# Adding the key tiles of the last three groups in float32 ahead of one float32 product

## The chip, the cores and the metric

The kernel runs on one core of a Trainium2 chip. The metric is the device time of one execution in microseconds (us); smaller is better. A core has TensorE (PE in the profile, with its weight loads as PEld), VectorE (DVE), ScalarE (ACT), GpSimd (POOL) and SyncE (SP). SP only issues DMAs here; POOL computes and issues DMAs.

## The reference

A cosine attention over 8 batches, 12 heads, 448 positions and 64 dimensions, followed by a two-layer network over the 3584 tokens:

```python
q_n = q / (np.linalg.norm(q, axis=-1, keepdims=True) + 1e-06)
k_n = k / (np.linalg.norm(k, axis=-1, keepdims=True) + 1e-06)
scores = np.matmul(q_n, k_n.transpose(0, 1, 3, 2)) / tau       # tau = 0.1
attn = np.exp(scores - np.max(scores, axis=-1, keepdims=True))
attn = attn / (np.sum(attn, axis=-1, keepdims=True) + 1e-09)
x = np.matmul(attn, v)                                         # to (3584, 768)
h = x @ w_in                                                   # 768 -> 2048
out = np.maximum(0.01 * h, h) @ w_out                          # 2048 -> 768
```

The kernel needs no maximum: the scores are bounded, and numerator and denominator carry the same factor. What this document turns on is the denominator, np.sum(attn): for each query the sum of the exps over all 448 keys.

## The kernel before, in words

**Slots, pairs, units, groups.** Two heads of one batch form a pair (48 pairs). The first 12 pairs (two batches) are done in an older way, in a part of the program written out by hand. From pair 12 on the work goes by *units*: a unit is two pairs, so four heads, and there are 18 of them. Units are gathered into ten *groups* of one or two units (line 186). The last three groups, 7, 8 and 9, are the units 12 and 13, 14 and 15, 16 and 17.

**A unit's key tiles.** A unit's 448 keys are cut into 7 tiles of 64. `quad_tiles` (line 406) makes one tile of scores with eight matmuls (L417), each on a strip of 64 rows by 32 columns of PE's array, into two PSUM banks; ScalarE takes the exp (L423) and writes a bf16 tile `pq[u, i]` of 128 x 2 x 448.

**Sums and products of a group.** `group_products(g, e)` (line 427) multiplies the exps of a group into two PSUM banks. With e = 0 or 1 the weights are columns of v, and the result is half of the attention's numerator. With e = None the weights are ones, and the result is the denominator. In each case there are 7 key tiles x 4 strips x 2 halves = 56 matmuls of 64x32 (L442), which accumulate over the tiles. `group_logs` (L451) and `group_inverse` (L454) turn the sums into reciprocals by way of a log and an exp on ScalarE, and `group_scale` (L467) multiplies the products by them on VectorE, into `xT`, the network's input.

**Visits.** The loop from line 892 on walks through the stream of all 18 x 7 = 126 key tiles, three in a *visit*, so 42 visits (0 to 41). A visit issues, in this order: the normalisation of one slot of a later unit (`normalise`, L253 to L260, on VectorE); its preparation; one key tile; a group's sums or products, if one is due; the other two key tiles; the load of the next group's v (`load_vq`, L202, two DMAs on POOL's queue); then matmuls of the network ("feed": `first`, L494, with its activation on ScalarE, L505, and `second`, L531, with its copy on VectorE, L541, and the DMA to the output), with `roots` of the next slot (L245, L246, ScalarE) ahead of the last piece of the feed. A group's sum comes in the visit after its last key tile, its two products in the two visits after that. Group 9 ends with the last visit, so its sum and its products stand behind the loop (lines 944 to 954), followed by the rest of the network.

**The preparation** (`prepare`, line 897) is: the transposition of the slot just normalised (L306, VectorE, then DMAs from SP), the load of a slot four further on (SP), then on POOL `hold` (L616, a copy of one column of the slot just normalised, which makes POOL wait for VectorE's L260) and `squares` of the slot two further on (L216, POOL), then on VectorE `sums` of the slot one further on (L232), which reads the squares that POOL made in an earlier visit. In visits that carry an e = 0 or 1 product the preparation stands behind that product.

**What sets the order.** The schedule is manual: each engine executes its instructions in the order of the program, and waits where one needs a result of another. The amount of feed in a visit comes from a small planner (lines 880 to 943) that counts the matmul columns of the network and of the e = 0 and 1 products. The eight PSUM banks are dealt in turn (`banks`, line 75): two for each key tile and each sum or product, one for each piece of the feed.

Of the kernel before, what the change touches and what calls it, by code (L numbers as in the profile page):

```python
# [8 lines left out]
F32 = mybir.dt.float32  # L9
BF16 = mybir.dt.bfloat16  # L10
AF = mybir.ActivationFunctionType
ALU = mybir.AluOpType
# [4 lines left out]
def kernel(  # L17
# [10 lines left out]
    nc = tc.nc  # L28
    B, H, S, D = q.shape
# [8 lines left out]
    NSLOT = B * NPAIR  # L38
    NQ = NPAIR // 2
# [8 lines left out]
    ctx.enter_context(tc.manual_schedule())  # L48
    cpool = ctx.enter_context(tc.tile_pool(name="consts", bufs=1))
    ldp = ctx.enter_context(tc.tile_pool(name="ld", bufs=4))  # L50
    vbp = ctx.enter_context(tc.tile_pool(name="vb", bufs=3))
    smp = ctx.enter_context(tc.tile_pool(name="small", bufs=3))
    qnp = ctx.enter_context(tc.tile_pool(name="qn", bufs=3))
    ttp = ctx.enter_context(tc.tile_pool(name="tt", bufs=2))
# [11 lines left out]
    gp = nc.gpsimd  # L66
# [8 lines left out]
    def banks(count, keep=None):  # L75
        lo, hi = (0, 8) if not deals["apart"] else (0, 4) if count == 2 else (4, 8)
        x = min(
            (i for i in range(lo, hi, count) if not set(range(i, i + count)) & set(kept.values())),
            key=lambda i: max(age[i : i + count]),
        )  # L80
        deals["n"] += 1
        age[x : x + count] = [deals["n"]] * count
        if keep:
            kept[keep] = x
        return ps[:, x] if count == 1 else ps[:, x : x + count]
# [26 lines left out]
    def main(x, b, h0, nh):  # L112
        return x[b, h0 : h0 + nh, 0:MAIN].rearrange("h (p t) d -> p h t d", t=3)
# [5 lines left out]
    def halves(x, w=D):  # L119
        return (  # L120
            x[:, 0 : 8 * w].rearrange("p (h t d) -> p h t d", h=2, d=w),
            x[:, 8 * w : 14 * w].rearrange("p (h t d) -> p h t d", h=2, d=w),
        )
# [45 lines left out]
    vb, vrb = {}, []  # L169

    def load_v(j):
        if j >= B * NQ:
            return
        b, jj = divmod(j, NQ)
        vb[j] = vbp.tile([128, 4, 3, D], BF16, name="v_b")
        gp.dma_start(out=vb[j], in_=main(v, b, 4 * jj, 4))

    def load_v_rem(b, heads=range(4)):
# [7 lines left out]
    GROUPS = [(6,), (7, 8), (9, 10), (11,)] + [(j, j + 1) for j in range(12, 24, 2)]  # L186
    assert [j for g in GROUPS for j in g] == list(range(NEWQ, B * NQ))
    UNITS = [
        (g, (2 * js[0] + x, 2 * js[-1] + x if len(js) == 2 else 2 * js[0] + 1))
        for g, js in enumerate(GROUPS) for x in range(len(js))  # L190
    ]
    vq = {}

    def load_vq(g):
# [14 lines left out]
    def squares(s, eng=gp, parts=(0, 1)):  # L209
        if s >= NSLOT:  # L210
            return
        sq = sqt[s % 3]
        if s >= OLD:
            sqs[s] = sq
            x = raw[s].rearrange("p (t d) -> p t d", d=D)
            gp.tensor_tensor(sq[:, :, :D], x, x, op=ALU.mult)  # L216
            return
        sqs[s] = halves(sq.rearrange("p t d -> p (t d)"), D + 1)
        for i in parts:
            x, y = raw[s][i], sqs[s][i]  # L220
            if eng is nc.scalar:
                nc.scalar.activation(y[..., :D], x, func=AF.Square)
            else:
                eng.tensor_tensor(y[..., :D], x, x, op=ALU.mult)  # L224

    def sums(s, parts=(0, 1)):
        if s >= NSLOT:
            return
        if s not in ss:
            ss[s] = smp.tile([128, 14], F32, name="ss")  # L230
        if s >= OLD:
            nc.vector.tensor_reduce(  # L232
                ss[s], sqs[s], axis=AX.X, op=ALU.add
            )
            return
        for i in parts:
            o = ss[s][:, 0:8] if i == 0 else ss[s][:, 8:14]
            nc.vector.tensor_reduce(  # L238
                o.rearrange("p (h t) -> p h t", h=2), sqs[s][i], axis=AX.X, op=ALU.add
            )  # L240
# [7 lines left out]
    qn = {}  # L248
# [80 lines left out]
    def pe_tile():  # L329
        return pep.tile([128, 2, S], BF16, name="pe")  # L330
# [71 lines left out]
            given_back((j, e))  # L402

    pq = {}

    def quad_tiles(which):

        tiles = []
        for u, i in which:
            sc = banks(2)  # L410
            tiles.append(sc)
            for strip in range(4):
                x = qkT[UNITS[u][1][strip // 2]]
                c0 = S + 64 * i + 32 * (strip % 2)
                for a in range(2):
                    rows = slice(64 * a, 64 * a + 64)
                    nc.tensor.matmul(  # L417
                        out=sc[32 * strip : 32 * strip + 32, a, :S], lhsT=x[rows, c0 : c0 + 32],
                        rhs=x[rows, 0:S], start=True, stop=True,
                    )  # L420
        for (u, i), sc in zip(which, tiles):
            pq[u, i] = pe_tile()
            nc.scalar.activation(out=pq[u, i], in_=sc[:, :, :S], func=AF.Exp, scale=inv_tau)  # L423
# [3 lines left out]
    def group_products(g, e):  # L427


        us = [u for u, (gg, _) in enumerate(UNITS) if gg == g]  # L430
        two = len(us) == 2
        po = banks(2)
        for i in range(7):
            for strip in range(4):
                for w in range(2):
                    x, a = strip // 2, strip % 2
                    rows = slice(64 * w, 64 * w + 64)
                    weights = ones[rows] if e is None else (
                        vq[g][rows, strip if two else a, i]
                        .rearrange("p (d e) -> p e d", e=2)[:, e if two else w ^ x]  # L440
                    )
                    nc.tensor.matmul(  # L442
                        out=po[32 * strip : 32 * strip + 32, w, :S],
                        lhsT=weights, rhs=pq[us[x if two else 0], i][rows, a, :],
                        start=(i == 0), stop=(i == 6),
                    )
        return po

    def group_logs(g, po):
        grb[g] = rbp.tile([128, 2, S], F32, name="rb")  # L450
        nc.scalar.activation(grb[g], po[:, :, :S], func=AF.Ln)  # L451

    def group_inverse(g):
        nc.scalar.activation(grb[g], grb[g], func=AF.Exp, scale=-1.0)  # L454
# [133 lines left out]
    nc.vector.memset(warm, 1.0)  # L588
    ones = cpool.tile([128, 32], BF16, name="ones")
    nc.vector.memset(ones, 1.0)  # L590
    ones_rem = cpool.tile([128, 2, 32], BF16, name="ones_rem")
    nc.vector.memset(ones_rem, 0.0)
    for i in range(2):
        nc.vector.memset(ones_rem[64 * i : 64 * i + 64, i], 1.0)
    for i in range(2):
        vrb.append(cpool.tile([128, NQ, 4, D], BF16, name=f"v_rem{i}"))
        nc.vector.memset(vrb[i], 0.0)
    id128 = cpool.tile([128, 128], BF16, name="id128")
    make_identity(nc, id128)
# [15 lines left out]
    def hold(x):  # L615
        gp.tensor_copy(out=seen, in_=x)  # L616
# [35 lines left out]
    for s in range(NPAIR):  # L652
        j = s // 2 - 1 if s >= 2 else None
# [39 lines left out]
        if s in (1, 2):  # L693
            load_v(s)
# [52 lines left out]
    s, j = NPAIR, NQ - 1  # L747
# [3 lines left out]
    po = banks(2)  # L751
# [135 lines left out]
        for n in range(len(visits))  # L887
    ]

    held = []  # L890
    fed = 0
    for n, tiles in enumerate(visits):
        s = preps.get(n, NSLOT)
        g, e = parts.get(n, (None, None))
        scaling = e is not None

        def prepare():
            if s < NSLOT:
                transposes(s)
                load_qk(s + 4)  # L900
                hold(qn[s][:, 6, 0, 0:1])
                squares(s + 2)
                sums(s + 1)

        normalise(s)
        if not scaling:
            prepare()
        quad_tiles(tiles[:1])
        if g is not None:
            po = group_products(g, e)  # L910
            if e is None:
                group_logs(g, po)
            else:
                group_scale(g, e, po)
        if scaling:
            prepare()
        quad_tiles(tiles[1:])
        if g is not None and e is None:
            group_inverse(g)
        for u, i in tiles:  # L920
            if i == 6 and u and UNITS[u][0] != UNITS[u - 1][0]:
                load_vq(UNITS[u][0])
        for c in marked:
            if at[c] == n:
                held += marked[c]
        level = min(
            (sum(loads[c] for c in loads if at[c] <= x) - fed + sum(side[n : x + 1])) / (x - n + 1)
            for x in range(n, len(visits))
        )
        share = (level - side[n]) / (4 if n == len(visits) - 1 else 1)  # L930
        now, done = [], 0
        while held:
            w = weight(held[0][0], held[0][1][0])
            if now and done + w / 2 > share:
                break
            now.append(held.pop(0)[1][1])
            done += w
        fed += done
        for fn in now[:-1]:
            fn()  # L940
        roots(s + 1)
        for fn in now[-1:]:
            fn()
    g = len(GROUPS) - 1
# [47 lines left out]
```

## Time and profile before

| what | value |
|---|---|
| median of 3 runs | 417.24 us (416.48 to 417.70) |
| the profiled execution: its own time | 416.43 us |
| the profiled execution: its span | 414.6 us |
| granted clock of PE | 1.00 |
| visits 28 to 41, by the chain | 245.5 to 344.3 us of the span |
| sum of group 7, 8, 9: start, duration in the chain | 278.19, 1.32; 314.67, 1.32; 344.27, 1.45 us |
| L423, one exp of a key tile (ScalarE) | 915 ns |
| L442 with ones: all 560 matmuls, busy | 15.1 us |
| POOL busy, 245.5 to 277.9 us | 8.5 of 32.4 us |

Times inside the profile count from the start of the span; the execution's own time is 1.8 us longer than its span. A line of the page's table of groups reads: code line, engine, operation, output and inputs, shape and count, then busy time and mean duration of one, then the idle time of that engine just before. The chain that ended last is found by going back from the last instruction, at each step to whatever released it; a piece of the chain is given by start, duration, engine and line. Matmuls are pipelined, so their single durations overlap, and the chain's pieces tell more about the rate.

### The profile page before, as it was taken

Reading aid. Unit: us, or ns where it says so; the run is one execution under the profiler, and the core shown is the slowest. Engines: PE = TensorE matmul, PEld = TensorE weight load, DVE = VectorE, ACT = ScalarE, POOL = GpSimd, SP = SyncE. Lnnn points to the kernel's source line nnn. Section 1 sums busy time; section 2 is a strip of 40 time slices with the busy share of each in tenths; the row PEclk is TensorE's granted clock in tenths of the full one; section 3 lists DMA queues with packets and bytes.
Section 4 is the critical chain, followed back from the end, with each engine's and each line's share of the span. In section 5 each row is a group of like instructions: output and inputs, shape, how many; then the busy total and the mean of one; then the engine's idle time right before and its main releaser. Section 6 shows DMA issues by size and latency. Waiting matters only on the chain.

```text
span 414.6 us, 11342 instructions
## 1 busy us (share of the span) xinstructions
PE 407.1 (98%) x4799; PEld 212.3 (51%) x4799; DVE 221.5 (53%) x387; ACT 250.2 (60%) x431; POOL 114.6 (28%) x149
## 2 busy tenths in 40 slices
PE   8899999999999999999999999999999999999997
PEld 3335555544555555544455555554445555654565
DVE  6977976855778556766474964464621301210022
ACT  5997876378657785668865688547764464004300
POOL 4875543433234132413331433122210000000000
PEclk9999999999999999999999999999999999999999
DMA  7999998775377851884275681742442100020022
GB/s 195 242 214 220 210 234 187 181 223 129 60 206 182 204 132 22 204 229 99 53 186 157 151 229 43 175 126 84 91 90 68 51 39 3 38 77 0 2 76 76
DMA packets 41964, 53.82 MB, mean 130 GB/s; under 512 B 12474, under 2 KB 32314, under 8 KB 41914
## 3 DMA queue, kind: packets, MB, share of 16 engines
q1 hardware_dynamic: 25738, 41.01, 35.0%
q0 software_dynamic: 15488, 11.80, 19.7%
q8 instruction: 37, 0.61, 0.6%
q10 hardware_dynamic: 688, 0.30, 0.2%
q14 instruction: 13, 0.11, 0.1%
HBM read 45.61 MB, written 11.01 MB: 137 GB/s over the span
## 4 chain that ended last, share of the span: by engine, by line
PE 87%; DMA 4%; ACT 3%; DVE 3%; POOL 2%; SPq 1%; issue 1%; POOLq 0%
PE ps L531 34%; PE ps L494 34%; PE ps L442 9%; PE ps L417 7%; ACT pe L355 2%; DMA qk_h<-in_k_dram 2%; PE ps L366 2%; DVE qn L270 1%; DMA xT<-in_k_dram 1%; DMA xT<-in_q_dram 1%; POOL sq L224 1%; PE ps L346 1%; POOL sq L216 1%; DVE ss L238 0%; SPq L131 0%
## 5 line engine op out<-in xcount | busy, mean ns | idle before, releaser
L531 PE MATMUL ps<-w_out_sb,hT 128*128 128x384 bf16 (+1 forms) x912 | 151.3, 324 | 0.3 <-DVE xT L397 0.3
L494 PE MATMUL ps<-xT,w_in_sb 128*128 128x384 bf16 (+1 forms) x768 | 151.1, 353 | 0.0
L423 ACT ACTIVATE pe<-ps 128x896 bf16<-128x896 f32 x126 | 108.9, 915 | 46.1 <-PE ps L417 46.1
L531 PEld LDWEIGHTS <-hT 128*128 128x128 bf16 x912 | 86.5, 98 | 64.3 <-issue 10.0
L494 PEld LDWEIGHTS <-w_in_sb 128*128 128x128 bf16 x768 | 72.6, 98 | 74.3 <-issue 9.7
L505 ACT ACTIVATE hT<-ps 128x384 bf16<-128x384 f32 (+1 forms) x128 | 67.4, 552 | 56.0 <-PE ps L494 55.0
L541 DVE COPY osb<-ps 128x384 f32<-128x384 f32 (+1 forms) x57 | 31.2, 548 | 100.7 <-PE ps L531 100.6
L216 POOL TENSOR_TENSOR sq<-qk_h 128x896 f32<-128x896 f32 x36 | 61.0, 1695 | 9.2 <-DMA qk_h<-in_k_dram 7.7
L616 POOL CAST seen<-qn 128x1 f32<-128x1 bf16 x46 | 8.5, 185 | 169.4 <-DVE qn L260 160.5
L260 DVE TENSOR_TENSOR qn<-qk_h,r 128x896 bf16<-128x896 f32 x36 | 42.4, 1176 | 1.2
L232 DVE TENSOR_REDUCE ss<-sq 128x14 f32<-128x910 f32 x36 | 38.0, 1054 | 1.1 <-POOL sq L216 1.1
L355 ACT ACTIVATE pe<-ps 128x896 bf16<-128x896 f32 x42 | 35.9, 917 | 1.8 <-PE ps L346 1.7
L417 PE MATMUL ps<-qkT 64*32 64x448 bf16 x1008 | 36.5, 353 | 0.0
L253 DVE TENSOR_REDUCE r<-norms 128x14 f32<-128x28 f32 x48 | 8.6, 178 | 48.3 <-ACT norms L246 47.7
L467 DVE TENSOR_TENSOR xT<-ps,rb 128x448 bf16<-128x448 f32 x32 | 18.4, 617 | 23.2 <-PE ps L442 21.5
L306 DVE STREAM_TRANSPOSE tt<-qn 128x448 f32<-128x448 f32 x36 | 29.6, 821 | 0.9
L442 PE MATMUL ps<-pe,vq 64*32 64x448 bf16 x1008 | 27.0, 349 | 0.0
L245 ACT ACTIVATE ss<-ss 128x14 f32<-128x14 f32 x48 | 10.3, 214 | 25.4 <-DVE ss L232 24.4
L417 PEld LDWEIGHTS <-qkT 64*32 64x32 bf16 x1008 | 13.1, 91 | 19.2 <-issue 14.5
L442 PEld LDWEIGHTS <-vq 64*32 64x32 bf16 x1008 | 14.5, 92 | 8.0 <-issue 0.3
L442 PE MATMUL ps<-pe,ones 64*32 64x448 bf16 x560 | 15.1, 349 | 0.0
L346 PE MATMUL ps<-qkT 64*64 64x448 bf16 (+1 forms) x132 | 12.9, 359 | 2.1 <-ACT pe L355 1.2
(53 smaller groups left out, 218.9 us busy)
## 6 DMA issues: line engine op xcount, KB each, us to landing
qk_h<-in_q_dram SPq DMA_DIRECT2D x36, 224.0 KB, 4.0
qk_h<-in_k_dram SPq DMA_DIRECT2D x36, 224.0 KB, 4.3
out_dram<-osb SPq DMA_DIRECT2D x20, 384.0 KB, 2.3
qkT<-tt SPq DMA_DIRECT2D x72, 56.0 KB, 3.3
qkT<-tt SPq DMA_DIRECT2D x36, 112.0 KB, 3.5
vq<-in_v_dram POOLq DMA_DIRECT2D x16, 224.0 KB, 5.0
w_in_sb<-in_moe_w_in_dram POOLq DMA_DIRECT2D x4, 768.0 KB, 11.2
w_out_sb<-in_moe_w_out_dram POOLq DMA_DIRECT2D x2, 1536.0 KB, 22.3
```

What stands on the lines that cost most here:

```text
L216: gp.tensor_tensor(sq[:, :, :D], x, x, op=ALU.mult)
L232: nc.vector.tensor_reduce(ss[s], sqs[s], axis=AX.X, op=ALU.add)
L260: nc.vector.tensor_tensor(qn[s].rearrange("p m d e -> p m e d"), raw[s].rearrange(f"p ({t[1:-1]} d) -> p m e d", e=n, d=D), r.rearrange(f" ...
L306: nc.vector.transpose(out=to.rearrange(("p g (c m) -> p m g c", "p g (m c) -> p m g c")[which], m=7), in_=qn[s].bitcast(F32).rearrange("p ...
L355: nc.scalar.activation(out=dst, in_=sc[:, :, :S], func=AF.Exp, scale=inv_tau)
L417: nc.tensor.matmul(out=sc[32 * strip : 32 * strip + 32, a, :S], lhsT=x[rows, c0 : c0 + 32], rhs=x[rows, 0:S], start=True, stop=True,)
L423: nc.scalar.activation(out=pq[u, i], in_=sc[:, :, :S], func=AF.Exp, scale=inv_tau)
L442: nc.tensor.matmul(out=po[32 * strip : 32 * strip + 32, w, :S], lhsT=weights, rhs=pq[us[x if two else 0], i][rows, a, :], start=(i == 0), ...
L494: nc.tensor.matmul(out=pm[:, :n], lhsT=w_in_sb[:, kt, m * 128 : (m + 1) * 128], rhs=xT[c // 2][:, kt, c0 : c0 + n], start=(done + i == 0), ...
L505: nc.scalar.activation(out=hT[c][:, m, :n], in_=pm[:, :n], func=AF.Prelu, alpha=0.01)
L531: nc.tensor.matmul(out=po2[:, : hi - lo], lhsT=hT[c][:, m, ts * 128 : (ts + 1) * 128], rhs=w_out_sb[:, m, half * HALF + lo : half * HALF + ...
L541: nc.vector.tensor_copy(out=o[:, cols], in_=po2[:, : hi - lo])
```

## The change

For the last three groups the denominator is no longer accumulated over seven key tiles by PE. The seven exp tiles of a unit are first added up element by element into one float32 tile `whole[u]` (128 x 2 x 448): six adds a unit, on GpSimd for units 12, 13 and 14 and on VectorE for units 15, 16 and 17. Then eight float32 matmuls, one for each strip and half, multiply this tile by float32 ones.

The adds of a visit's key tiles are issued behind its last two key tiles; the first add of a unit waits until the group of the unit two before is summed, since there are two float32 tiles. In the visits that carry adds, `hold` and `squares` move behind the adds. To make room, the v tiles of the old part and the two float32 tiles share one buffer, and the float32 ones are written over the identity matrix, which is no longer used then. `ADDED` is 7 and `BY_VECTOR` 15.

```diff
-    vbp = ctx.enter_context(tc.tile_pool(name="vb", bufs=3))
...
-        vb[j] = vbp.tile([128, 4, 3, D], BF16, name="v_b")
+        vb[j] = v_old[:, j % 3]
...
+    ADDED = len(GROUPS) - 3
+    BY_VECTOR = len(UNITS) - 3
...
+    whole, due, summed = {}, [], set()
+
+    def add_up():
+        for u, i in list(due):
+            if i == 1:
+                if UNITS[u - 2][0] >= ADDED and UNITS[u - 2][0] not in summed:
+                    return
+                whole[u] = sum_of[u % 2]
+            due.remove((u, i))
+            eng = gp if u < BY_VECTOR else nc.vector
+            eng.tensor_tensor(
+                whole[u], pq[u, 0] if i == 1 else whole[u], pq[u, i], op=ALU.add
+            )
...
         po = banks(2)
+        if e is None and g >= ADDED:
+            summed.add(g)
+            for strip in range(4):
+                for w in range(2):
+                    rows = slice(64 * w, 64 * w + 64)
+                    nc.tensor.matmul(
+                        out=po[32 * strip : 32 * strip + 32, w, :S], lhsT=ones_f[rows],
+                        rhs=whole[us[strip // 2]][rows, strip % 2, :], start=True, stop=True,
+                    )
+            return po
...
+    shared = cpool.tile([128, 3840], BF16, name="shared")
+    v_old = shared[:, :2304].rearrange("p (j h t d) -> p j h t d", j=3, t=3, d=D)
+    sum_of = [
+        shared[:, 1792 * i : 1792 * (i + 1)].bitcast(F32).rearrange("p (a c) -> p a c", c=S)
+        for i in range(2)
+    ]
...
-        vrb.append(cpool.tile([128, NQ, 4, D], BF16, name=f"v_rem{i}"))
+        lo = 2304 + 768 * i
+        vrb.append(shared[:, lo : lo + 768].rearrange("p (j g d) -> p j g d", g=4, d=D))
...
+    ones_f = id128.bitcast(F32)[:, 0:32]
+    nc.vector.memset(ones_f, 1.0)
...
+        adding = [(u, i) for u, i in tiles if i and UNITS[u][0] >= ADDED]
...
-                hold(qn[s][:, 6, 0, 0:1])
-                squares(s + 2)
+                if not adding:
+                    hold(qn[s][:, 6, 0, 0:1])
+                    squares(s + 2)
                 sums(s + 1)
...
         quad_tiles(tiles[1:])
+        due += adding
+        add_up()
+        if adding and s < NSLOT:
+            hold(qn[s][:, 6, 0, 0:1])
+            squares(s + 2)
```

## The prediction

> **What bounds the kernel.** I read the page's busy shares first, then the chain that ended last, then what TensorE (PE) waited for.
>
> ```profile
> PE 407.1 (98%) x4799; PEld 212.3 (51%) x4799; DVE 221.5 (53%) x387; ACT 250.2 (60%) x431; POOL 114.6 (28%) x149
> ...
> PE 87%; DMA 4%; ACT 3%; DVE 3%; POOL 2%; SPq 1%; issue 1%; POOLq 0%
> ```
>
> PE is busy in 98% of the span and carries 87% of the chain. All that PE ever waited for another engine is this:
>
> ```profile
> PE ps L605 <- DVE pe L588: 1.7, 1, 1.7
> PE ps L346 <- ACT pe L355: 1.2, 5, 0.3
> PE ps L346 <- DVE qkT L325: 0.8, 1, 0.8
> PE ps L284 <- DVE qn L270: 0.6, 2, 0.4
> PE ps L531 <- DVE xT L397: 0.3, 1, 0.3
> ```
>
> None of these lines belongs to the visits (L417, L442): from the first visit on, PE never waits. So there a microsecond of PE is a microsecond of time, and another engine costs something only if it becomes late enough to make PE wait. The chain in order of time (start, duration, what) shows one visit that sums a group, and the stage after the last visit:
>
> ```profile
> 277.88 0.31 PE ps L417 x8
> 278.19 1.32 PE ps L442 x56
> 279.51 0.38 PE ps L417 x16
> ...
> 334.41 9.86 PE ps L494 x60
> 344.27 1.45 PE ps L442 x56
> 345.71 4.01 PE ps L494 x24
> ...
> 354.55 15.60 PE ps L531 x96
> ```
>
> The x56 pieces at 278.19 and 344.27 are sums over the key tiles (weights of ones) of groups 7 and 9; group 8's lies at 314.67, 1.32 us too. From these pieces come two rates. Seven rounds of eight matmuls, each on its own 64x32 strip of the array, take 1.32: eight strips side by side take **0.189 us** for 448 columns. And 96 matmuls of 384 columns that all use the same 128x128 array take 15.60, so 0.1625 each, 0.423 ns a column, which is again 0.189 for 448. So strips that differ run beside each other, and matmuls on one and the same piece of the array follow one another at full streaming time, their weight loads (98 ns each in L531's row) hidden.
>
> **What goes from PE.** Three sums of 56 matmuls: 3 x 1.32 = 3.96 us. All of it is on the chain.
>
> **What comes to PE.** Three times eight float32 products of 64 rows, 32 weights, 448 columns. The built program has 4679 matmuls for 4799: 168 go and 48 come, so each float32 product is two pairs of weight load and matmul. They stand product by product, both matmuls of one product on the same strip, then the next strip. No row of this trace has a float32 matmul, so I bound P, the time of the sixteen. Below: all sixteen at the bf16 pace of strips side by side, 16 x 0.189 / 8 = 0.38. Above: none beside another, and each with twice the bytes. A bf16 column is 2 bytes per row, a float32 one is 4; at L442's bytes per time one matmul takes 2 x 0.189 = 0.379, and sixteen 6.06. The value I take lies between and follows from the two rates above and the order in the program: the second matmul of a product waits for the first, being on its strip (0.379); the next strip's first may run beside it; but its second must wait for its own first. Eight steps of 0.379 and one more to drain: **P = 9 x 0.379 = 3.41 us**. That rests on matmuls starting in program order.
>
> The Trainium skill, "TensorE: Matmul & The Clock Gate" (Part 3, "What overlaps and what doesn't"), says that matmuls start and end strictly in program order; by it the pairs chain as above. Its page "TensorEngine Tiling (Array Packing)" (Key Properties) says that tiles operate independently and in parallel; read to the letter, that gives rival B below. No row of this trace has two matmuls of one small strip in succession, so neither is settled here.
>
> Sum for PE: 3 x (3.41 - 1.32) = **+6.27 us**.
>
> **What comes to GpSimd (POOL).** Eighteen adds for units 12, 13 and 14 (six each). No row has this add; the nearest is the square, L216, a two-input operation on 128x896: 1.68 us in these visits. Below that I have 1.04 for 512 elements (L224), above it this:
>
> ```profile
> 62.02 1.17 DVE L260 TENSOR_TENSOR qn<-qk_h,r 128x896 bf16<-128x896 f32 x1
> 62.53 2.16 POOL L216 TENSOR_TENSOR sq<-qk_h 128x896 f32<-128x896 f32 x1 [3.64 <-DMA qk_h<-in_k_dram]
> 66.26 1.68 POOL L216 TENSOR_TENSOR sq<-qk_h 128x896 f32<-128x896 f32 x1 [1.44 <-DMA qk_h<-in_q_dram]
> ```
>
> The columns are start, duration, engine and line (in brackets, POOL's idle time before). The square at 62.53 began while VectorE (DVE) multiplied two inputs, and took 2.16 where an undisturbed one takes 1.68. Range 1.04 to 2.16; I take 1.68. The Trainium skill, "SBUF — State Buffer" (Who interferes with whom), has a DVE instruction with two SBUF inputs and a GpSimd instruction that reads SBUF block one another; the 0.48 us here agrees in kind, and it speaks against the change, since now the adds run under L260, whereas the squares stood behind it.
>
> Do the adds hold PE up? Group 7's product (278.19) needs unit 12 for its first eight matmuls and unit 13 for the rest, which by my chain begin 4 x 0.379 later, at 279.7. POOL works in order. Unit 13's first add can start when the exps of visit 30 are done, about 265.2 (three exps of 0.9 beginning at 261.5, with two waits). Then follow: one add (to 266.9), the two vq loads (1.27, to 268.2), three adds (to 273.2), the hold and square of visit 31 (0.18 + 1.68, to 275.1), two adds (to 278.5). That is 1.2 us early. The cover is gone when an add takes over 1.9 us; beyond that each 0.1 us costs PE 0.6. At 2.16 it would be 279.7 against 281.3, a stall of 1.6. So I cost it at **nothing**. It happens once only: unit 14 is summed five visits on.
>
> **What moves.** In visits 28, 29 and 31 to 34 hold and square now stand behind two or three adds, which wait for the exps of their own visit. The tightest is the square of visit 31, which ends at 270.1 in the trace and about 275.1 then: DVE's L232 reads it in visit 32's preparation (274.65), so L232 slips some 0.5 us, and with it ScalarE's roots (275.74) and the copy L541 queued behind (275.63). The roots' reader, L253, comes at 278.39: 2 us are left. The vq loads slip from 258.0 to about 267 and land 5 us later; their first reader is the product at 288.1. SP's queue has the same order as before. So nothing again: the cover is these gaps, and without them L541 and the exps would hold PSUM banks and so PE.
>
> **What comes to DVE.** Eighteen adds at L260's 1.18 (two float32 SBUF inputs, the same 896 elements): 21 us from visit 35 on, where DVE is busy little (16.2 of 36.5 us from 277.9 to 314.4, and 5.7 of 29.9 from there to 344.3, by the table of stretches). The adds wait for exps, and behind them wait L541 and L467. The last visit's three exps end at 336.6, so the last add near 338; its product comes at 344.27, behind 9.86 us of L494. Group 8's last add ends near 311 for a product at 314.67. **Nothing.** The first part of the kernel keeps its order and waits; the memset of the float32 ones is one DVE instruction of under 0.1 us.
>
> **The sum.** The profiled execution took 416.43 (span 414.6 and 1.8 around it); with 6.27 it is 422.7. The median of the runs shown, 417.24, is 0.81 above that execution, so for a median I predict **423.5**.
>
> **Rivals.** A measurement of this kernel can tell about 0.3% (1.25 us) from no change.
>
> A, as forecast: P between 3.0 (the eight first matmuls hidden, 8 x 0.379) and 4.24 (a weight load of 0.092 added to each of nine steps): 417.24 + 5.1 to + 8.8, so 422.4 to 426.0. For it: L531's one-after-another rate and the order in the program. Chance 0.58.
>
> B, the other side: different strips run ahead of one another, so that the sixteen overlap eight by eight. Place: the three products. P = 2 x 0.379 = 0.76, price 3 x (0.76 - 1.32) = -1.7, so 415.6. It turns to a gain where P is under 1.32. For it: L442 keeps eight strips full; against: there each strip's next matmul comes eight instructions later, here at once. Chance 0.20.
>
> C, bytes do not count, only columns, and pairs chain: P = 9 x 0.189 = 1.70, +1.2, so 418.4. Chance 0.07.
>
> D, float32 matmuls do not run beside others at all: P = 6.06, +14.2, so 431.5. For it: nothing in the trace; against it only that L442's do. Chance 0.10.
>
> E, the change adds what A does, and POOL's adds last 2.16: PE waits 1.6 at group 7, so 425.1. For it: the row at 62.53; against: L260 is 1.18 in visits of 6 us. Chance 0.05.
>
> Slower: A, D, E, 0.73. Same: C, 0.07. Faster: B, 0.20. The range goes from B to the top of A, 415.3 to 426.5, and leaves out D. A's own range is 422.4 to 426.0.
>
> **What would show it.** Right: three pieces of about 3.4 us in the chain where 1.32 stood, the second matmul of a product starting 0.38 after its first; no PE wait for POOL or DVE; POOL adds of 1.7. Wrong: pieces under 1.3 us (B) or of 6 (D); a PE wait at 278 released by POOL (E); PE waits at L417 or L531 after 265 for banks, which would mean that late squares or waiting adds block L541 or the roots.

## The result and the profile after

The change takes 420.49 us (median of 6 executions, 419.29 to 421.14) against 416.94 before (six executions, the three shown ahead of the forecast among them): ratio **1.0071**, 95% interval 1.0054 to 1.0088. That is 3.0 us by the ratio of the executions (3.55 between the two medians). It is slower, as forecast, but by about half of the 6.3 us forecast, and for other reasons. Two later measurements of the same kernel gave 1.0033 (1.0011 to 1.0055) and 1.0046 (1.0029 to 1.0063).

The busy shares and the chain of the changed kernel (in its listing L452 is the float32 product, L416 the adds, L431 the key tiles, L466 the bf16 products, L518 and L555 the network, L565 its copies, L261 the normalisation):

```profile
span 417.5 us, 11153 instructions
...
PE 404.6 (97%) x4663; PEld 210.6 (50%) x4679; DVE 243.2 (58%) x406; ACT 250.5 (60%) x431; POOL 151.5 (36%) x167
...
PE 81%; DVE 5%; POOL 4%; DMA 4%; ACT 3%; issue 2%; SPq 1%; POOLq 0%; DVEq 0%
```

PE is busy 2.5 us less than before (407.1), yet the span is 2.9 us longer: PE did less and waited more. POOL, 2% of the chain before, is 4% now. (The page lacks the records of 16 of the 4679 matmuls.) What PE waited for, in total, times, longest:

```profile
PE ps L452 <- POOL shared L416: 1.9, 1, 1.9
PE ps L636 <- DVE pe L612: 1.7, 1, 1.7
PE ps L285 <- DVE qn L271: 1.4, 1, 1.4
PE ps L347 <- ACT pe L356: 1.2, 5, 0.3
PE ps L555 <- DVE r L255: 1.2, 1, 1.2
...
PE ps L518 <- DVE osb L565: 0.3, 1, 0.3
```

The first line is new and lies where the forecast had no cost: group 7's product waits for GpSimd's adds. The last is new too. The wait of 1.2 at L555 lies ahead of the visits (below). The chain at the sums of groups 8 and 9, which do not wait for an add:

```profile
317.84 0.31 PE ps L431 x8
318.15 0.75 PE ps L452 x16
318.90 0.38 PE ps L431 x16
```

```profile
342.93 4.71 PE ps L518 x29
347.64 0.91 PE ps L452 x16
348.55 3.52 PE ps L518 x21
```

Sixteen float32 matmuls take **0.75 us**, where 1.32 stood and 3.41 was forecast; behind the 128x128 matmuls of the network 0.91, where 1.45 stood. PE in order of time at group 8 (start, duration of the run of instructions, count) shows why:

```profile
317.77 0.38 PE L431 MATMUL ps<-qkT 64*32 64x448 bf16 x8
317.97 0.56 PE L452 MATMUL ps<-shared,id 64*32 64x448 f32 x8
```

These are the rows in flight between 318.0 and 318.1: eight of the sixteen. Between 318.7 and 318.8 it is the other eight:

```profile
318.34 0.56 PE L452 MATMUL ps<-shared,id 64*32 64x448 f32 x8
318.72 0.37 PE L431 MATMUL ps<-qkT 64*32 64x448 bf16 x8
```

Eight start together at 317.97 and eight at 318.34, and the next key tile follows at 318.72: two rounds in 0.75, so **0.375 us** each. Each matmul does take about twice the 0.189 us of a bf16 one, but all eight strips run beside each other, though the program gives both matmuls of a strip in succession.

**A stretch that all profiles share.** To compare single executions I use the stretch from the start of visit 28's network matmuls (x42) to the start of those behind group 9's sum (the x24 of 4.01 us). Before it is 247.56 to 345.71, so 98.15 us. After it is 248.79 to 348.55, so 99.76: **+1.61**. Two more profiles of the changed kernel gave 99.78 and 99.76. What is left of the longer span, 1.23 us, lies ahead of visit 28. There, profiles of kernels whose programs are the same differ by up to 2.2 us (visit 28's network begins between 247.20 and 249.43): PE's first use of the second half of w_out waits for its load, and the following matmuls start between 70.1 and 71.9 us (70.49 before, 71.72 after).

The 1.61 divides so: three sums, 0.57 + 0.57 + 0.54 gained; the visit of group 7 lost 2.82 (from its first key tile to its network 4.26 us, where 1.44 would do without a wait); the last visit lost 0.43. Together +1.57. Of the 2.82, PE stands idle for 1.88; the rest goes because the product now runs in two halves, each of which fills only four of the eight strips.

**Group 7's wait.** POOL in order of time, in visits 30 to 33:

```profile
264.74 1.89 POOL L416 TENSOR_TENSOR shared<-shared,pe 128x896 f32<-128x896 f32 x1
266.58 1.89 POOL L416 TENSOR_TENSOR shared<-pe 128x896 f32<-128x896 bf16 x1
268.40 1.27 POOL L203 DMA_DIRECT2D vq<-in_v_dram  x2
269.68 5.84 POOL L416 TENSOR_TENSOR shared<-shared,pe 128x896 f32<-128x896 f32 x3
275.46 1.09 POOL L647 CAST seen<-qn 128x1 f32<-128x1 bf16 x1
276.51 1.67 POOL L217 TENSOR_TENSOR sq<-qk_h 128x896 f32<-128x896 f32 x1
278.15 3.84 POOL L416 TENSOR_TENSOR shared<-shared,pe 128x896 f32<-128x896 f32 x2
```

POOL never rests. An add takes 1.89, not 1.68 (1.88 also at 252.25, while VectorE does nothing), and hold (L647, 0.18 before) takes 1.09. Unit 13's sum is finished at 282.0; allowing for the 1.23 us by which this execution entered the visits late, the forecast's 278.5 becomes 279.7. The difference of 2.3 is six adds of 0.2 more, 1.2, and 0.9 of hold; the rest is the first add, which begins at 266.58, behind unit 12's last, where the forecast, moved by 1.23, has 266.4. VectorE in the same time:

```profile
268.18 1.31 DVE L261 TENSOR_TENSOR qn<-qk_h,r 128x896 bf16<-128x896 f32 x1
...
274.11 2.43 DVE L261 TENSOR_TENSOR qn<-qk_h,r 128x896 bf16<-128x896 f32 x1
...
280.64 2.37 DVE L261 TENSOR_TENSOR qn<-qk_h,r 128x896 bf16<-128x896 f32 x1
```

L261 reads two tensors, as the add does; under POOL's adds it takes 2.4 where 1.18 is usual, and hold waits for it. And PE:

```profile
279.24 0.92 PE L452 MATMUL ps<-shared,id 64*32 64x448 f32 x8
282.04 0.58 PE L452 MATMUL ps<-shared,id 64*32 64x448 f32 x4 [1.88 <-POOL shared L416]
```

The eight matmuls of unit 12 are soon done, the rest waits.

**The last visit.** VectorE's adds stand ahead of the copy L565 that frees a PSUM bank for PE's L518:

```profile
335.89 2.29 DVE L416 TENSOR_TENSOR shared<-shared,pe 128x896 f32<-128x896 f32 x2
338.10 0.55 DVE L565 COPY osb<-ps 128x384 f32<-128x384 f32 x1
```

PE resumes at 338.70.

### The profile page after: what moved, and what is told of

It is laid out like the page before. It is cut to its first block, busy times and chain, and to the rows that moved or that the text cites. A ratio compares the mean times of both kernels' runs of the same rounds, so it can differ in the third digit from the quotient of the medians.

```text
span 417.5 us, 11153 instructions
## 1 busy us (share of the span) xinstructions
PE 404.6 (97%) x4663; PEld 210.6 (50%) x4679; DVE 243.2 (58%) x406; ACT 250.5 (60%) x431; POOL 151.5 (36%) x167
## 4 chain that ended last, share of the span: by engine, by line
PE 81%; DVE 5%; POOL 4%; DMA 4%; ACT 3%; issue 2%; SPq 1%; POOLq 0%; DVEq 0%
PE ps L518 33%; PE ps L555 30%; PE ps L466 8%; PE ps L431 6%; ACT pe L356 2%; DMA qk_h<-in_k_dram 2%; PE ps L367 2%; POOL shared L416 2%; DMA xT<-in_k_dram 1%; DVE qn L271 1%; POOL sq L225 1%; DMA xT<-in_q_dram 1%; POOL sq L217 1%; DVE shared L416 1%; PE ps L347 1%
## 5 line engine op out<-in xcount | busy, mean ns | idle before, releaser
L555 PE MATMUL ps<-w_out_sb,hT 128*128 128x384 bf16 (+1 forms) x912 | 151.3, 324 | 1.2 <-DVE r L255 1.2
L518 PE MATMUL ps<-xT,w_in_sb 128*128 128x384 bf16 (+1 forms) x754 | 150.2, 352 | 1.1 <-DVE osb L565 0.3
L555 PEld LDWEIGHTS <-hT 128*128 128x128 bf16 x912 | 86.5, 98 | 65.2 <-issue 10.0
L518 PEld LDWEIGHTS <-w_in_sb 128*128 128x128 bf16 x768 | 72.7, 98 | 75.0 <-issue 10.7
L565 DVE COPY osb<-ps 128x384 f32<-128x384 f32 (+1 forms) x57 | 31.1, 547 | 85.0 <-PE ps L555 85.0
L647 POOL CAST seen<-qn 128x1 f32<-128x1 bf16 x46 | 11.3, 245 | 129.3 <-DVE qn L261 120.8
L261 DVE TENSOR_TENSOR qn<-qk_h,r 128x896 bf16<-128x896 f32 x36 | 45.5, 1264 | 1.2
L233 DVE TENSOR_REDUCE ss<-sq 128x14 f32<-128x910 f32 x36 | 38.0, 1055 | 2.7 <-POOL sq L217 2.7
L431 PE MATMUL ps<-qkT 64*32 64x448 bf16 x1008 | 37.1, 353 | 0.0
L416 POOL TENSOR_TENSOR shared<-shared,pe 128x896 f32<-128x896 f32 x15 | 28.5, 1902 | 2.7 <-ACT pe L437 1.9
L466 PE MATMUL ps<-pe,vq 64*32 64x448 bf16 x1008 | 27.0, 349 | 0.0
L431 PEld LDWEIGHTS <-qkT 64*32 64x32 bf16 x1008 | 13.2, 91 | 19.9 <-issue 15.2
L466 PEld LDWEIGHTS <-vq 64*32 64x32 bf16 x1008 | 14.5, 93 | 8.0 <-issue 0.3
L416 DVE TENSOR_TENSOR shared<-shared,pe 128x896 f32<-128x896 f32 x15 | 16.3, 1088 | 1.9 <-ACT pe L437 0.7
```

Source lines behind the costliest of these rows:

```text
L233: nc.vector.tensor_reduce(ss[s], sqs[s], axis=AX.X, op=ALU.add)
L261: nc.vector.tensor_tensor(qn[s].rearrange("p m d e -> p m e d"), raw[s].rearrange(f"p ({t[1:-1]} d) -> p m e d", e=n, d=D), r.rearrange(f" ...
L416: eng.tensor_tensor(whole[u], pq[u, 0] if i == 1 else whole[u], pq[u, i], op=ALU.add)
L431: nc.tensor.matmul(out=sc[32 * strip : 32 * strip + 32, a, :S], lhsT=x[rows, c0 : c0 + 32], rhs=x[rows, 0:S], start=True, stop=True,)
L466: nc.tensor.matmul(out=po[32 * strip : 32 * strip + 32, w, :S], lhsT=weights, rhs=pq[us[x if two else 0], i][rows, a, :], start=(i == 0), ...
L518: nc.tensor.matmul(out=pm[:, :n], lhsT=w_in_sb[:, kt, m * 128 : (m + 1) * 128], rhs=xT[c // 2][:, kt, c0 : c0 + n], start=(done + i == 0), ...
```

## The experiments

The theory (T): the float32 product gains 1.7 us, group 7 loses 2.8 to GpSimd's queue, the last visit 0.4 to VectorE's. All diffs are against the changed kernel unless said otherwise. Each ratio is to executions of the kernel before on the same chip. The last column is the shared stretch in the one profiled execution, minus its 98.15 before. In e1, e9 and e13 the sums are not those of the attention: they leave out adds or double the sums, to show what these cost.

| kernel | ratio to before (95%) | stretch |
|---|---|---|
| the change, three times | 1.0071, 1.0033, 1.0046 | +1.61, +1.63, +1.61 |
| e1, no adds | 0.9954 (0.9939 to 0.9968) | -1.67 |
| e2, adds unused | 1.0004 (0.9992 to 1.0016) | +0.44 |
| e3, halves | 1.0023 (1.0010 to 1.0036) | +1.17 |
| e4, layout alone | 0.9993 (0.9984 to 1.0002) | +0.01 |
| e5, two groups | 0.9969 (0.9957 to 0.9981) | -1.10 |
| e6, squares first | 1.0141 (1.0122 to 1.0160) | +5.96 |
| e7, later product | 1.0014 (1.0004 to 1.0023) | +0.45 |
| e8, later, resplit | 1.0005 (0.9988 to 1.0023) | +0.01 |
| e9, twice | a single execution | +1.07 |
| e11, group 7 later | 0.9966 (0.9952 to 0.9981) | -1.29 |
| e12, no hold | 1.0043 (1.0027 to 1.0059) | +1.33 |
| e13, two adds fewer | 0.9974 (0.9961 to 0.9986) | -1.04 |

**e1, the product without the adds.**

```diff
-            eng = gp if u < BY_VECTOR else nc.vector
-            eng.tensor_tensor(
-                whole[u], pq[u, 0] if i == 1 else whole[u], pq[u, i], op=ALU.add
-            )
...
     nc.vector.memset(ones_f, 1.0)
+    for i in range(2):
+        nc.vector.memset(sum_of[i], 1.0)
```

> The float32 products and the moved hold and squares stay; the adds are left out: the products read two float32 tiles that VectorE fills with ones once, in place of the sums over the key tiles. Theory T: a float32 product takes 0.75 us where 1.32 stood, nothing waits for an add, so 3 x 0.57 = 1.7 us under the kernel before (ratio 0.996). Rival R1, the shared buffer costs 1.2 us ahead of the first visit by itself: 0.5 us under (0.999). Rival R2, float32 products disturb PE in a way that the profile does not show: not below before.

Measured 0.9954, and 1.67 us less in the stretch. The float32 product is a gain of its full size; R1 and R2 fall.

**e2, the adds without the product.**

```diff
         if e is None and g >= ADDED:
             summed.add(g)
+        if False:
             for strip in range(4):
```

> All eighteen adds on GpSimd and eighteen on VectorE as in the change, but the three sums are made by 56 bf16 matmuls each as before, so nothing waits for a finished tile of sums. Theory T: PE does not wait for GpSimd at group 7; what is left is up to 0.4 us in the last visit, where copies stand behind VectorE's adds: 0 to 0.5 us over before (1.000 to 1.001). R1: 1.2 to 1.7 over (1.003 to 1.004). Rival R3, the late squares and the blocked normalisation cost PE time themselves: 2 us over or more (1.005).

Measured 1.0004, +0.44 in the stretch: the last visit. The adds, the late squares and the stretched normalisation cost PE nothing else as long as no product waits for them. R1 and R3 fall.

**e3, one unit of each group for each engine.**

```diff
-            eng = gp if u < BY_VECTOR else nc.vector
+            eng = gp if u % 2 == 0 else nc.vector
```

> As the change, but in each of the three groups the first unit (12, 14, 16) is added up by GpSimd and the second (13, 15, 17) by VectorE. Theory T: GpSimd has a whole unit of time more before group 7 is summed, so the wait of 2.8 us goes; 1.7 us gained, 0.4 lost in the last visit or nothing: 1.3 to 1.7 us under before (0.996 to 0.997). R1: 0.1 to 0.5 under (0.999 to 1.000). Were VectorE's adds of unit 13 as late as GpSimd's: as the change (1.007).

A miss: 1.0023. GpSimd is in time, but in visits 30 to 32, which are full of copies, VectorE's adds hold these up. VectorE and then PE in order of time:

```profile
271.38 3.47 DVE L416 TENSOR_TENSOR shared<-shared,pe 128x896 f32<-128x896 f32 x3
274.77 1.01 DVE L565 COPY osb<-ps 128x384 f32<-128x384 f32 x2
```

```profile
272.98 0.76 PE L431 MATMUL ps<-qkT 64*32 64x448 bf16 x24
275.37 1.95 PE L555 MATMUL ps<-w_out_sb,hT 128*128 128x384 bf16 x11 [1.63 <-DVE osb L565]
```

Three adds in a row, two copies behind them, and PE 1.63 us without a bank. The wait has moved from GpSimd's adds to VectorE's copies. About 0.7 us more goes at group 7's product: VectorE's last adds of unit 13 end at 281.44, and the product, begun at 281.05, waits for them.

**e4, the shared buffer alone**, against the kernel before:

```diff
-        vb[j] = vbp.tile([128, 4, 3, D], BF16, name="v_b")
+        vb[j] = v_old[:, j % 3]
...
-        vrb.append(cpool.tile([128, NQ, 4, D], BF16, name=f"v_rem{i}"))
+        lo = 2304 + 768 * i
+        vrb.append(shared[:, lo : lo + 768].rearrange("p (j g d) -> p j g d", g=4, d=D))
```

> The kernel before with one part of the change alone: the v tiles of the old part lie in the shared buffer, no adds and no float32 product. Theory T: the 1.2 us ahead of the first visit in the one profiled execution is the landing of a weight load, which differs from execution to execution: same as before (1.000, within 0.001). R1: 1.2 us over (1.003).

Measured 0.9993. The layout costs nothing, although this profile too began its visits late (82.38, where the kernel before has 80.95 and the change 82.19): that offset belongs to the execution.

**e5, groups 8 and 9 alone.**

```diff
-    ADDED = len(GROUPS) - 3
+    ADDED = len(GROUPS) - 2
...
-            eng = gp if u < BY_VECTOR else nc.vector
+            eng = gp if u in (14, 17) else nc.vector
```

> The change for groups 8 and 9 alone (group 7 keeps its bf16 sum); GpSimd adds up units 14 and 17, VectorE 15 and 16. Theory T: no sum is waited for, VectorE's adds in the last visit no longer stand ahead of copies, so 2 x 0.57 = 1.1 us under the kernel before (ratio 0.997). Rival R3 (the blocked normalisation and the late squares cost PE time): 1.000 or above.

As T has it: 0.9969, -1.10 in the stretch, and no wait in the visits. This version is faster than both kernels.

**e6, hold and squares in their old place.**

```diff
-                if not adding:
-                    hold(qn[s][:, 6, 0, 0:1])
-                    squares(s + 2)
+                hold(qn[s][:, 6, 0, 0:1])
+                squares(s + 2)
...
-        if adding and s < NSLOT:
-            hold(qn[s][:, 6, 0, 0:1])
-            squares(s + 2)
```

> The change with hold and squares back in their old place, ahead of the adds. Theory T: GpSimd's work until unit 13 is summed stays the same sum, so PE still waits at group 7, within 1 us of the 2.8 us of the change: ratio 1.005 to 1.008 to the kernel before. Rival R4, the moved squares are the cause of the wait: it goes, 0.997.

A miss for both: 1.0141. A second square (visit 32's) now comes ahead of unit 13's last two adds, and more of the adds run beside a normalisation: the three and the two that took 5.84 and 3.84 us in the change take 6.58 and 4.60. Unit 13's sum is finished 2.7 us later than in the change. What PE waited for, and the table of the two stretches about that wait (duration, PE busy, ..., granted clock in the third column from the end):

```profile
PE ps L452 <- POOL shared L416: 4.6, 1, 4.6
```

```profile
270.00:283.00 13.00, 9.14 (x85) 4.66 (x83) 11.49 (x15) 4.31 (x8) 12.77 (x8) 1.00 0.66 159
283.00:293.00 10.00, 9.28 (x54) 3.61 (x55) 0.87 (x1) 5.64 (x8) 8.04 (x6) 0.83 0.14 49
```

After a wait of 4.6 us the granted clock (PE's share of its full speed) is 0.83 in the mean: 0.50 from 283.9 to 287.2, then 1.00. The 36 matmuls that follow the product take 8.47 us, 7.88 before. So the move of the squares was no cost; it spared 4.4 us, 2.7 of them wait and the rest the slower product and matmuls behind it. R4 falls.

**e7, the products of groups 7 and 8 behind half of the visit's network matmuls; e8, the same with unit 17 on GpSimd.**

```diff
+        later = g is not None and e is None and g >= ADDED
...
+        half = len(now) // 2 if later else 0
+        for fn in now[:half]:
+            fn()
+        if later:
+            group_logs(g, group_products(g, None))
+            group_inverse(g)
+            add_up()
+        for fn in now[half:-1]:
+            fn()
```

> The change, but in the visits that sum group 7 and group 8 the float32 product, its log and its inverse stand behind half of the visit's network matmuls instead of ahead of them (group 7: three pieces, 3.9 us later). Theory T: the wait of 2.8 us for GpSimd's adds is covered, 1.7 us gained and 0.4 lost in the last visit: 1.3 us under before (0.997). If the loss has another cause than this wait: 1.005 or more. If the later log and inverse hold up ScalarE's exps: between the two.

> As the kernel with the later product, and GpSimd adds up units 12, 13, 14 and 17, VectorE 15 and 16, so that no VectorE add stands ahead of a copy in the last visit. Theory T: the 0.4 us there go too: 1.7 us under before (0.996). If that wait is not from VectorE's adds: as the kernel with the later product.

Two misses: e7 is 1.0014, e8 1.0005, where T had 0.997 and 0.996. The wait at group 7 is gone in both, and 0.44 separates them in the stretch, the last visit's. But in e8 the whole gain of 1.7 us is missing. Laid beside e1, its chain is 0.35 us longer in the visit of group 7 and 1.3 in those of group 8 and after: the product of group 8 takes 0.91 amid the network matmuls, and in the next visit PE waits for a bank again. The chain, then VectorE:

```profile
318.30 0.91 PE ps L452 x16
...
322.23 1.40 PE ps L466 x56
...
323.91 0.56 DVE osb L565
```

```profile
319.31 1.09 DVE L416 TENSOR_TENSOR shared<-pe 128x896 f32<-128x896 bf16 x1 [0.41 <-PE ps L452]
320.50 3.49 DVE L416 TENSOR_TENSOR shared<-shared,pe 128x896 f32<-128x896 f32 x3
323.91 0.55 DVE L565 COPY osb<-ps 128x384 f32<-128x384 f32 x1
```

The later product of group 8 makes unit 16's adds later (they share its tile), and a copy stands behind them. So e11, with e8's split of the units, moves group 7's product alone.

**e11**, against e8:

```diff
-        later = g is not None and e is None and g >= ADDED
+        later = g is not None and e is None and g == ADDED
```

> GpSimd adds up units 12, 13, 14 and 17, VectorE 15 and 16; only group 7's float32 product stands behind half of its visit's network matmuls, group 8's stays where the change has it. Theory T: nothing is waited for; 1.7 us gained, less 0.3 for leaving and re-entering the small strips in mid feed: 1.4 us under before (ratio 0.9967). If the later product itself is what cost in the two kernels with it: 1.000.

Measured 0.9966: all three sums in float32, no wait in the visits. With e5 it is the fastest of the kernels that make the attention's own sums; the intervals do not tell the two apart.

**e9, each product twice, in e1.**

```diff
-                        rhs=whole[us[strip // 2]][rows, strip % 2, :], start=True, stop=True,
+                        rhs=whole[us[strip // 2]][rows, strip % 2, :], start=True, stop=False,
                     )
+                    nc.tensor.matmul(
+                        out=po[32 * strip : 32 * strip + 32, w, :S], lhsT=ones_f[rows],
+                        rhs=whole[us[strip // 2]][rows, strip % 2, :], start=False, stop=True,
+                    )
```

> The kernel without adds (products read constant tiles), and each float32 product is issued twice in succession, the second accumulating on the first: four matmuls in a row on the same strip, then the next strip; the sums are twice as large. If each strip works through its own matmuls and strips run beside each other whatever stands between them in the program: 4 x 0.373 = 1.5 us a group where the kernel without adds takes 0.75. If matmuls start in program order, a strip's chain holds back the next strip: 8 x 3 x 0.373 + 0.373 = 9.3 us a group. If only a pair is taken together: between the two.

```profile
278.80 0.97 PE ps L448 x16
279.77 0.70 PE ps L452 x16
```

```profile
278.61 1.15 PE L448 MATMUL ps<-shared,id 64*32 64x448 f32 x16
279.37 1.15 PE L452 MATMUL ps<-shared,id 64*32 64x448 f32 x16
```

Thirty-two matmuls in 1.67 us, four in a row on every strip: near 4 x 0.375 = 1.50, far from 9.3 (the first eight start spread over 0.2 us here). And although the source gives L448 and L452 in turn, product by product, all sixteen of L448 start before the first of L452. Strips work beside each other whatever stands between them in the program, to this depth. The order meant is the source's; no profile lists the order of the built program. A reordering within a unit when the program is built would not do as the cause: in the change, group 7 runs the eight of unit 12 as two rounds while unit 13's wait, so unit 12's second round stands ahead of unit 13's first, and yet at group 8 the first rounds of both units start together.

**e10 and e14, the change again.**

> The changed kernel unaltered, for a second profile. Theory T: ahead of the visits it differs from the first profile by up to 1.5 us either way (the landing of w_out). At group 7 PE waits again for GpSimd's adds. Theory T2: where that wait is longer than in the first profile (1.9 us in one piece), the granted clock falls below 1.00 in the stretch after it, as it did with the squares first (4.6 us, then 0.83), and that is why most executions of the change lie 0.5 to 1.9 us above the profiled one. If the clock stays 1.00 with a total above 420, T2 falls.

> The changed kernel unaltered, on the chip of the three kernels beside it. By the two earlier measurements: 1.003 to 1.007.

Both show the same wait, 1.9 us, and the same stretch within 0.02. T2 is not borne out by these profiles: the clock after the 1.9 us wait is 1.00 in both. The execution profiled in e14 has a granted clock of 0.996 over its whole span, but it lost it from 20.3 to 23.7 us (0.50 there), long before the first add.

**e12, no hold.**

```diff
         if adding and s < NSLOT:
-            hold(qn[s][:, 6, 0, 0:1])
             squares(s + 2)
```

> The change without hold in the visits that carry adds, so that GpSimd's squares there do not wait for VectorE's normalisation L261, which GpSimd's adds stretch from 1.2 to 2.4 us. Theory T: in visit 31's preparation GpSimd stood about 1.0 us waiting for that; the wait of PE at group 7 gets shorter by about 1.0 us: 0.0025 under the unaltered change. If the adds alone set the end of unit 13: as the change.

A miss: 1.0043 beside 1.0046 for the change on the same chip, 0.3 us less in the stretch, where 1.0 was expected.

```profile
268.95 5.83 POOL L416 TENSOR_TENSOR shared<-shared,pe 128x896 f32<-128x896 f32 x3
274.74 2.57 POOL L217 TENSOR_TENSOR sq<-qk_h 128x896 f32<-128x896 f32 x1
277.27 3.84 POOL L416 TENSOR_TENSOR shared<-shared,pe 128x896 f32<-128x896 f32 x2
```

The square, free to start at once, now meets the normalisation itself and takes 2.57 for 1.68. The 0.9 us moved from hold to the square: it is the meeting of the two engines that costs, not the order.

**e13, two adds fewer.**

```diff
             due.remove((u, i))
+            if u == 13 and i > 4:
+                continue
```

> The change with the last two adds of unit 13 left out (key tiles 5 and 6 are missing in its sum). Theory T: GpSimd is done with unit 13 some 3.8 us earlier, PE does not wait at group 7, 1.7 us gained and 0.4 lost in the last visit: 1.3 us under before (0.997). If something other than GpSimd's queue holds up group 7: over before.

Measured 0.9974, and no wait at group 7. So GpSimd's queue is what PE waits for.

## Why the prediction was wrong, and what in it was right

The time came out slower, and inside the stated range, but by luck: the term that was to make the kernel slower made it faster, and a wait that was put at nothing outweighed the gain. Rival A, the forecast itself, did not happen.

**What bounds the kernel: right.** A microsecond of PE in the visits is a microsecond of time; e1 regained 1.67 of the 1.68 us that the three products are shorter.

**P, the sixteen matmuls: wrong, and the largest error.** The term was 3.41 us and measured 0.75. Right in it was the time of one matmul (0.379 forecast, 0.375 measured). Wrong was the step "its second must wait for its own first" as a bar to the next strip, which the text rested on matmuls starting in program order. The eight strips run their first matmuls together and then their second ones, so the step takes two rounds and not nine. Rival B had this (0.76), at a chance of 0.20. The Trainium skill, "TensorE: Matmul & The Clock Gate" (Part 3, "What overlaps and what doesn't"), has matmuls strictly in program order, start and end; here that does not hold across strips, by group 8's starts and by e9. "TensorEngine Tiling (Array Packing)" (Key Properties), by which tiles work independently, agrees. Against the forecast's +6.27 the sums gave -1.68. (Rival C's +1.2 is 1.14 by its own figures; its total of 418.4 stands.)

**GpSimd "at nothing": wrong.** The lateness was reckoned, with its tipping point (1.9 us an add), but the add was priced at the square's 1.68 and took 1.89; the cover counted on 1.5 us from the slow product that did not exist; and the collision with L260 was seen in the row at 62.53 and then left out of the chain, where it cost 0.9. Cost in place of nothing: 2.82 us. Rival E named the place, at 0.05 and tied to A; B and E together were not among the rivals, and that is what happened in kind, with a dearer wait than E's 1.6. The Trainium skill, "SBUF — State Buffer" (Who interferes with whom), says that a VectorE instruction with two SBUF inputs and a GpSimd instruction that reads SBUF block one another; L261 at 2.43 in the change and the square at 2.57 in e12 agree.

**The moved squares: right.** e2 shows that they cost nothing, e6 that leaving them ahead would have cost 4.4 us more. The room was smaller than reckoned, though: L233 in visit 32, L232 before, slipped by 2.3 us (278.22 less the 1.23, for 274.65), not by 0.5.

**VectorE "at nothing": nearly.** 0.43 us in the last visit, by the very copies named; in e3 the same mechanism took 1.6.

**The early part: right in the program,** as e4 shows.

**What stays open.** The shared stretch accounts for +1.6 us in each of three profiles, and the second and third measurement (about 1.4 and 1.9 us by their ratios) agree with it. The first gave 3.0, and what made that set dearer was not found. A granted clock of 0.996 is part of it: three of its six executions show one. In the three sets of the change together it is 6 of 22 executions, against 5 of the 91 of the kernel before that ran beside the experiments. The one such execution that was profiled, e14's, lost its clock ahead of all adds; whether others lost theirs after the wait at group 7 is not shown. One of the dear executions of the first set (420.87 us) has a clock of 1.00, so there is something else as well.

## What to carry to other kernels

Work taken off the bounding engine is gained only if what replaces it is finished before that engine asks for it: reckon the helper's queue item by item, with everything else that stands in it, and price an unseen operation at the dear end of its rows where the slack is small. Adds placed in an in-order queue also delay what stands behind them, here the copies that free PSUM; before moving work between engines, look which copies are behind it. Where the helper is late, a later place for the consumer in a visit (e11) or leaving out the one group with short visits (e5) took the same change from between 1.003 and 1.007 to 0.997.

## What was not expected of the hardware

- A float32 product of 64x32 strips took four times one round of eight bf16 strips (0.75 against 0.189 us), and less than seven bf16 rounds (1.32): two matmuls of 0.375 us on each strip. The Trainium skill, "FP8 and Floating Point Precision" (TensorE Precision Notes), has four passes for true float32; the measured ratio agrees.
- GpSimd's add of 128x896 takes 1.89 us, its square of one tensor 1.68.
- PE's granted clock fell to 0.50 for about 3.3 us after a wait of 4.6 us (e6, from 283.9), and stayed 1.00 after waits of 1.9 (three profiles of the change). The length of one wait is not all: in e14 it fell to 0.50 at 20.3 us, just behind a wait of 1.34, and the first profile of the change has the same wait there (1.35) without a fall.
- A sum of small strips costs 0.13 to 0.16 us more behind 128x128 matmuls than behind small strips (0.91 against 0.75; 1.45 against 1.32 in the kernel before).
